# Order of the first attention job's start in a fused attention and expert kernel

## The chip, the cores and the metric

The kernel runs on one core of a Trainium2 chip. The metric is the device time of one execution in microseconds (us), as the median of several runs. The kernel before took 746.56 us (three runs, 745.12 to 747.57).

## What is computed

The reference is attention over 16 heads, followed by two feed-forward layers in float32. Cut to what matters:

```python
# q, k, v: (2, 8, 576, 64)
scores = scale * np.matmul(q, k.transpose(0, 1, 3, 2))
thresh = np.max(scores, axis=-1, keepdims=True) - tau
scores = np.where(scores >= thresh, scores, -1000000000.0)
scores = scores - np.max(scores, axis=-1, keepdims=True)
attn = np.exp(scores)
attn = attn / (np.sum(attn, axis=-1, keepdims=True) + 1e-09)
x = np.matmul(attn, v)                  # then as (1152, 512)
x = np.maximum(np.maximum(x @ w1, x @ w2), x @ w3) @ w_out
p = domain_probs / (domain_probs.sum(-1, keepdims=True) + 1e-09)
for e in range(4):
    out += p[:, e:e + 1] * (np.maximum(x @ m_w1[e], 0.0) @ m_w2[e])
```

The weights w1, w2, w3 and w_out come as 64-bit floats.

## The kernel before

Every float32 operand of a matmul is split in a high part (rounded by a copy on ScalarE) and the rest (a subtraction on VectorE or GpSimd), and products are summed over these parts. The program has three stretches. In the first (`attention_fast`) the eight heads of the first batch element are done as four jobs of two heads. In the second the other eight heads (`attention_slow`) are woven into the matmuls of the first three weight matrices. The rest is the expert layers, which are matmuls of one line, L832.

A job loads q, k and v of two heads (`load_job`, lines 129 and 130; the 64 rows over the 512 of a head are the tiles `qrem`, `krem`, `vrem`). `prep` transposes keys and queries on TensorE and splits them (K on ScalarE, L169, and VectorE, L171; QS on ScalarE, L178). The first job has its own forms: `load_first` (lines 140 to 142) and `prep_first`. There `head(h)` copies keys (L206), splits queries (L207, L208), transposes both (L214, L216) and splits the keys (L219, L221) and scales the queries (L220); between `head(0)` and `head(1)` the remaining 64 rows go through L226 to L237.

A job has nine steps (tiles of 128 query rows of a head, and one step for the remaining rows of both heads). A step's scores are four matmuls (`qk`, L301; eight for the step of the remaining rows). Then VectorE takes the negated row maximum (`peak`, L312) and a threshold (`limit`, L315), ScalarE the exponential (`power`, L319), VectorE the thresholding with the row sum (`weigh`, L324), GpSimd the division (`norm`, L332). TensorE transposes the result (`turn`, L342), it is split (`cut_hi` on ScalarE, L372, L375 and L379; `cut_lo`, L388 to L400) and multiplied by V (`gather`, L418). There are two PSUM buffers for scores, two of the kind T, and two of the kind U.

Beside this, `stream.flush(when)` writes out the preparation of weight blocks that is due at a count of matmul columns `when`. For 64-bit weights this is: load the words (L638, 512 KB each), exponent on ScalarE (L646), clamp on GpSimd (L656), and three integer operations on VectorE (L653, L659, L664). Then the block is stored for a second pass (L670) and split (L626, L630). Three such blocks are prepared during the first attention stretch with their own, early due times (`LAGS_FIRST`). `load_probs` loads the domain probabilities, which `norm_probs` uses long after.

In the first stretch the order of instructions on each engine is set by a scheduler of the language, which goes by priority and by its own idea of when something is ready. `tc.issue_after(x)` makes the instructions written inside it, on the engine of `x`, stand behind `x` in that engine's order. It adds no semaphore. Each engine executes its own list strictly in order. From the first L832 on, the order of the program text holds on TensorE, VectorE, ScalarE and GpSimd.

## Time and profile before

| what | before |
|---|---|
| median of three runs | 746.56 us |
| the profiled execution, its own time | 749.09 us |
| span of the profiled execution | 747.3 us |
| TensorE busy (share of the span) | 715.7 us (96%) |
| VectorE busy | 378.3 us (51%) |
| ScalarE busy | 339.0 us (45%) |
| GpSimd busy | 392.4 us (53%) |
| first L832 matmul | at 107.66 us |

The profile is one execution taken by the hardware profiler. Its views are the page (totals), a table of stretches (busy time of every engine between two times), the timeline (instructions in order of time), the waits and the chain of work that ended last. PE is TensorE, PEld its weight load, DVE is VectorE, ACT ScalarE, POOL GpSimd, SP the queue that issues most DMAs. A time in brackets with an arrow is how long the engine had been idle before an instruction, and what ended that.

### The profile page before, as it was taken

Reading aid. Unit: us, or ns where it says so; the run is one execution under the profiler, and the core shown is the slowest. Engines: PE = TensorE matmul, PEld = TensorE weight load, DVE = VectorE, ACT = ScalarE, POOL = GpSimd, SP = SyncE. Lnnn points to the kernel's source line nnn. Section 1 sums busy time; section 2 is a strip of 40 time slices with the busy share of each in tenths; the row PEclk is TensorE's granted clock in tenths of the full one; section 3 lists DMA queues with packets and bytes.
Section 4 is the critical chain, followed back from the end, with each engine's and each line's share of the span. In section 5 each row is a group of like instructions: output and inputs, shape, how many; then the busy total and the mean of one; then the engine's idle time right before and its main releaser. Section 6 shows DMA issues by size and latency. Waiting matters only on the chain.

```text
span 747.3 us, 11716 instructions
## 1 busy us (share of the span) xinstructions
PE 715.7 (96%) x4103; PEld 636.4 (85%) x4103; DVE 378.3 (51%) x900; ACT 339.0 (45%) x716; POOL 392.4 (53%) x435
## 2 busy tenths in 40 slices
PE   4798999999899999999999999999999999999997
PEld 3787889777688788888888899999998998998996
DVE  6798988775265765766766421112222222222222
ACT  5688984444544655465454412333321321321320
POOL 5789785777554555564564524544623522522520
PEclk9799999999999999999999999999999999999999
DMA  6702006876724124122322233223412313312303
GB/s 183 227 22 49 1 1 187 261 226 204 199 78 113 59 73 122 57 73 57 86 61 66 71 113 85 68 58 91 132 50 85 99 43 85 104 45 77 113 2 71
DMA packets 89369, 71.01 MB, mean 95 GB/s; under 512 B 24158, under 2 KB 75358, under 8 KB 89310
## 3 DMA queue, kind: packets, MB, share of 16 engines
q1 hardware_dynamic: 88860, 69.96, 32.7%
q8 instruction: 33, 0.54, 0.3%
q10 hardware_dynamic: 418, 0.30, 0.2%
q14 instruction: 26, 0.21, 0.1%
q0 software_dynamic: 32, 0.00, 0.0%
HBM read 61.59 MB, written 8.65 MB: 94 GB/s over the span
## 4 chain that ended last, share of the span: by engine, by line
PE 77%; DVE 5%; ACT 5%; POOL 5%; issue 3%; DMA 3%; SPq 1%; POOLq 0%; ACTq 0%; DVEq 0%
PE ps L832 63%; PE u L418 5%; PE s L301 4%; PE t L342 3%; POOL a L630 2%; DVE st_negm L312 1%; DMA vrem<-in_v_dram 1%; ACT em L319 1%; DMA words<-in_moe_w_dram 1%; POOL b L656 1%; PE u L175 1%; DMA krem<-in_k_dram 1%; DVE raw L664 1%; ACT a L626 1%; PE t L388 1%
## 5 line engine op out<-in xcount | busy, mean ns | idle before, releaser
L630 POOL TENSOR_TENSOR a<-raw,a 128x512 fp32r<-128x512 f32 (+1 forms) x116 | 145.1, 1256 | 163.6 <-ACT a L626 160.3
L832 PE MATMUL ps<-b,hh 128*128 128x512 f32 x576 | 184.3, 393 | 0.0
L832 PEld LDWEIGHTS ps<-b,hh 128*128 128x128 f32 x576 | 107.3, 188 | 20.4
L782 ACT ACTIVATE hh<-ps 128x320 fp32r<-128x320 f32 (+1 forms) x96 | 46.8, 488 | 152.3 <-PE ps L832 151.9
L832 PE MATMUL ps<-b,hl 128*128 128x512 f32 x288 | 113.1, 393 | 0.0
L832 PE MATMUL ps<-y1h,a 128*128 128x320 f32 x512 | 112.8, 309 | 0.0
L630 POOL TENSOR_TENSOR b<-raw,b 128x512 fp32r<-128x512 f32 x64 | 82.8, 1296 | 53.4 <-ACT b L626 53.4
L785 DVE SCALAR_TENSOR_TENSOR hl<-ps,hh 128x320 fp32r<-128x320 f32 (+1 forms) x96 | 53.4, 556 | 108.9 <-ACT hh L782 108.8
L626 ACT ACTIVATE a<-raw 128x512 fp32r<-128x512 f32 (+1 forms) x116 | 69.4, 612 | 58.8 <-PE ps L832 19.1
L801 DVE SCALAR_TENSOR_TENSOR acc<-ps,pr,acc 128x512 f32<-128x512 f32 x63 | 47.2, 749 | 80.4 <-PE ps L832 80.3
L832 PE MATMUL ps<-y0h,a 128*128 128x512 f32 x256 | 85.1, 403 | 0.8 <-POOL a L630 0.8
L832 PEld LDWEIGHTS ps<-y1h,a 128*128 128x128 f32 x512 | 85.4, 188 | 0.3
L319 ACT ACTIVATE em<-s,st_negm 128x576 f32<-128x576 f32 x72 | 53.3, 744 | 70.9 <-DVE st_negm L312 70.7
L332 POOL TENSOR_SCALAR em<-em,st_r,even 128x576 f32<-128x576 f32 x70 | 57.5, 824 | 43.2 <-DVE st_r L331 41.6
L832 PE MATMUL ps<-y1l,a 128*128 128x320 f32 x256 | 79.1, 309 | 0.0
L312 DVE TENSOR_REDUCE st_negm<-s 128x1 f32<-128x576 f32 x72 | 54.1, 753 | 48.9 <-PE s L301 48.4
L301 PE MATMUL s<-K,QS 128*128 128x288 f32 x320 | 59.7, 315 | 6.4 <-DVE em L324 3.2
L832 PE MATMUL ps<-x1h,a 128*128 128x320 f32 x288 | 63.4, 309 | 0.0
L324 DVE SCALAR_TENSOR_TENSOR em<-s,st_thr,em 128x576 f32<-128x576 f32 x72 | 58.2, 812 | 9.9 <-ACT em L319 7.8
L832 PEld LDWEIGHTS ps<-b,hl 128*128 128x128 f32 x288 | 54.1, 188 | 10.0
L301 PEld LDWEIGHTS s<-K,QS 128*128 128x128 f32 x320 | 49.8, 197 | 11.3 <-issue 6.0
L832 PEld LDWEIGHTS ps<-y0h,a 128*128 128x128 f32 x256 | 47.8, 191 | 9.6 <-POOL a L630 1.2
(129 smaller groups left out, 1271.1 us busy)
## 6 DMA issues: line engine op xcount, KB each, us to landing
raw<-in_moe_w_dram SPq DMA_DIRECT2D x128, 256.0 KB
words<-in_moe_w_dram SPq DMA_DIRECT2D x18, 512.0 KB
kept_w<-raw SPq DMA_DIRECT2D x18, 256.0 KB
raw<-kept_w SPq DMA_DIRECT2D x18, 256.0 KB
kraw<-in_k_dram SPq DMA_DIRECT2D x30, 128.0 KB
words<-in_moe_w_out_dram SPq DMA_DIRECT2D x8, 384.0 KB
vraw<-in_v_dram SPq DMA_DIRECT2D x8, 256.0 KB
qraw<-in_q_dram SPq DMA_DIRECT2D x7, 256.0 KB
```

The costliest lines, as they stand in the source:

```text
L301: nc.tensor.matmul(st.s[:, kh, 0:HS], lhsT=l, rhs=r, start=i == 0, stop=i == len(terms) - 1)
L312: nc.vector.tensor_reduce(out=st.stat["negm"], in_=views(st)[0], op=ALU.max, axis=AX.XY, negate=True)
L319: nc.scalar.activation(out=ev, in_=sv, func=AF.Exp, bias=st.stat["negm"])
L324: nc.vector.scalar_tensor_tensor(out=ev, in0=sv, scalar=st.stat["thr"], in1=ev, op0=ALU.is_ge, op1=ALU.mult, accum_out=st.stat["sum"])
L332: last = (nc.vector if swift else nc.gpsimd).tensor_scalar(out=em, in0=em, scalar1=re, scalar2=even, op0=ALU.mult, op1=ALU.add)
L418: at["valued"] = nc.tensor.matmul(pv, lhsT=l, rhs=r, start=i == 0, stop=i == len(terms) - 1)
L626: nc.scalar.activation(out=b["hi"], in_=b["raw"], func=AF.Copy)
L630: nc.gpsimd.tensor_tensor(out=b["lo"], in0=b["raw"], in1=f32(b["hi"]), op=ALU.subtract)
L782: nc.scalar.activation(out=hs[f][0][:, a:z], in_=ps, func=AF.Relu)
L785: nc.vector.scalar_tensor_tensor(out=hs[f][1][:, a:z], in0=ps, scalar=0.0, in1=f32(hs[f][0][:, a:z]), op0=ALU.max, op1=ALU.subtract)
L801: nc.vector.scalar_tensor_tensor(out=accs[t], in0=ps, scalar=pe, in1=accs[t], op0=ALU.mult, op1=ALU.add)
L832: nc.tensor.matmul(ps, lhsT=l, rhs=r, start=i == 0, stop=i == count - 1)
```

## The change

The remaining rows and the second head of the first job stand behind the first head's last scaling and last subtraction; the second head also stands behind the remaining rows' first instructions. The first step's `peak` and `power` are written right after `prep_first`. Everything that is written after that and before the end of the third pass of the loop (the second job's loads, the values, the weight preparation, later steps) stands, on its engine, behind these and behind each of the first steps' `power` and `weigh`. The due times of the early weight preparation are flushed in pieces (-53000, then -45900, -42500 and -READY after the first three steps' `weigh`) where it was all flushed before the first step. The values of the first job are queued one step later; the second job's `prep` starts one step later, and its loads are written before the loop. The domain probabilities' loads stand behind the last job's loads.

```diff
@@ load_job @@
-                nc.sync.dma_start(out=r[:, x, :], in_=src[b, 2 * p:2 * p + 2, MAIN:S, :])
+                last = nc.sync.dma_start(out=r[:, x, :], in_=src[b, 2 * p:2 * p + 2, MAIN:S, :])
             job.raw[nm] = (t, r)
+        at["loaded"] = last
+        return last
@@ prep_first @@
-            nc.scalar.activation(out=QS[:, qo:qo + MAIN], in_=tq, func=AF.Copy, scale=SCALE)
-            nc.vector.tensor_tensor(out=K2[:, ko:ko + MAIN], in0=tk, in1=f32(d1), op=ALU.subtract)
-
-        head(0)
+            sq = nc.scalar.activation(out=QS[:, qo:qo + MAIN], in_=tq, func=AF.Copy, scale=SCALE)
+            return sq, nc.vector.tensor_tensor(out=K2[:, ko:ko + MAIN], in0=tk, in1=f32(d1), op=ALU.subtract)
+
+        behind = ExitStack()
+        for x in head(0):
+            behind.enter_context(tc.issue_after(x.ins))
         split(QN[:, 2 * NC:], qr, kr[:, None])
...
-        nc.scalar.activation(out=k1r, in_=trk, func=AF.Copy)
-        nc.vector.tensor_tensor(out=k2r, in0=trk, in1=f32(k1r), op=ALU.subtract)
+        x1 = nc.scalar.activation(out=k1r, in_=trk, func=AF.Copy)
+        x2 = nc.vector.tensor_tensor(out=k2r, in0=trk, in1=f32(k1r), op=ALU.subtract)
         yield
-        head(1)
+        for x in (turned, x1, x2):
+            behind.enter_context(tc.issue_after(x.ins))
+        job.ready = head(1)
+        behind.close()
@@ attention_fast @@
         load_job(jobs[0], "v")
+        stream.flush(-53000)
         start = prep_first(jobs[0])
         next(start)
         qk(steps[0])
         for _ in start:
             pass
-        stream.flush(-READY)
-        back.add(values(jobs[0]))
+
+        begun = ExitStack()
+        for x in (peak(steps[0]), power(steps[0]), *jobs[0].ready):
+            begun.enter_context(tc.issue_after(x.ins))
+
+        begun.enter_context(tc.issue_after(load_job(jobs[1]).ins))
...
-                if st.r == LOAD_A:
+                if st.r == LOAD_A and i:
                     load_job(jobs[st.j + 1])
-                if st.r == PREP_A:
+                if st.r == PREP_A + (st.j == 0):
                     front.add(prep(jobs[st.j + 1]))
-            if st:
+            if i and st:
                 peak(st)
...
-            if nxt:
-                power(st)
+            if i and nxt:
+                raised = power(st)
+                if i <= 2:
+                    begun.enter_context(tc.issue_after(raised.ins))
+                if i == 1:
+                    back.add(values(jobs[0]))
...
-                weigh(st)
+                weighed = weigh(st)
+                if i <= 2:
+
+                    begun.enter_context(tc.issue_after(weighed.ins))
+                    stream.flush((-45900, -42500, -READY)[i])
...
+            if i == 2:
+                begun.close()
@@ at the end @@
-    plan.at(0, load_probs)
+    def load_probs_late():
+        with tc.issue_after(at["loaded"].ins):
+            load_probs()
+
+    plan.at(0, load_probs_late)
```

The names below are those of the program's tiles: kraw, krem, qraw, qrem, vraw and vrem are loaded rows, QN split queries, K and QS transposed keys and queries, s scores, st_negm, st_thr and st_sum a step's maximum, threshold and sum, em the exponentials, words, t, b and raw the weight preparation. The lines of the changed kernel are shifted by 2 to 26.

VectorE, from behind the scalar constant of tau at the very start, before:

```order
L206 COPY krem<-krem 128x64
L900 TENSOR_SCALAR even<-neg 128x1
L902 SCALAR_TENSOR_TENSOR ntau<-neg,tau_c 128x1
L208 TENSOR_TENSOR QN<-qraw,QN 128x4x64
L208 TENSOR_TENSOR QN<-qrem,QN 128x64
L206 COPY kraw<-kraw 128x4x64
L221 TENSOR_TENSOR K_135<-u,K_134 128x512
L208 TENSOR_TENSOR QN<-qraw,QN 128x4x64
L653 TENSOR_SCALAR t<-words 128x512
L232 TENSOR_TENSOR K_135<-t,K_134 128x2x64
L221 TENSOR_TENSOR K_135<-u,K_134 128x512
L653 TENSOR_SCALAR t<-words 128x512
```

and of the change, from the first head's query subtraction on:

```order
L210 TENSOR_TENSOR QN<-qraw,QN 128x4x64
L223 TENSOR_TENSOR K_137<-u,K_136 128x512
L208 COPY krem<-krem 128x64
L210 TENSOR_TENSOR QN<-qrem,QN 128x64
L236 TENSOR_TENSOR K_137<-t,K_136 128x2x64
L208 COPY kraw<-kraw 128x4x64
L210 TENSOR_TENSOR QN<-qraw,QN 128x4x64
L319 TENSOR_REDUCE st_negm<-s 128x1
L223 TENSOR_TENSOR K_137<-u,K_136 128x512
L322 TENSOR_SCALAR st_thr<-st_negm,ntau 128x1
L331 SCALAR_TENSOR_TENSOR em,st_sum<-s,st_thr,em 128x576
L675 TENSOR_SCALAR t<-words 128x512 x2
```

The copy of krem moved behind the first head's subtractions, the first maximum moved ahead of the second head's key subtraction, and both operations on words moved behind the first step's `weigh`; the second step's maximum comes next.

ScalarE, from the first query split on, before:

```order
L207 ACTIVATE QN<-qraw 128x4x64
L207 ACTIVATE QN<-qrem 128x64
L219 ACTIVATE K_134<-u 128x512
L207 ACTIVATE QN<-qraw 128x4x64
L220 ACTIVATE QS<-u 128x512
L231 ACTIVATE K_134<-t 128x2x64
L646 ACTIVATE b<-words 128x512
L219 ACTIVATE K_134<-u 128x512
L235 ACTIVATE QS<-t 128x2x64
L646 ACTIVATE b<-words 128x512
L220 ACTIVATE QS<-u 128x512
L246 ACTIVATE V<-vraw 128x8x64
```

and of the change:

```order
L209 ACTIVATE QN<-qraw 128x4x64
L221 ACTIVATE K_136<-u 128x512
L222 ACTIVATE QS<-u 128x512
L209 ACTIVATE QN<-qrem 128x64
L235 ACTIVATE K_136<-t 128x2x64
L209 ACTIVATE QN<-qraw 128x4x64
L242 ACTIVATE QS<-t 128x2x64
L326 ACTIVATE em<-s,st_negm 128x576
L221 ACTIVATE K_136<-u 128x512
L222 ACTIVATE QS<-u 128x512
L668 ACTIVATE b<-words 128x512 x2
L326 ACTIVATE em<-s,st_negm 128x576
```

The first exponential moved ahead of the second head's copies, of the exponents and of the values; before, it stood behind V and both VR.

SP, from the third load of words on, before:

```order
L638 DMA words<-in_moe_w_dram 128x4x256
L129 DMA qraw<-in_q_dram 128x2x256
L130 DMA qrem<-in_q_dram 128x1x64
L129 DMA kraw<-in_k_dram 128x4x64 x2
L130 DMA krem<-in_k_dram 128x1x64
L129 DMA kraw<-in_k_dram 128x4x64 x2
L130 DMA krem<-in_k_dram 128x1x64
L670 DMA kept_w_0_201<-raw 128x512
L638 DMA words<-in_moe_w_dram 128x4x256 x2
L129 DMA vraw<-in_v_dram 128x2x256
L130 DMA vrem<-in_v_dram 128x1x64
L847 DMA pr<-in_moe_domain_probs_dram 128x16
```

and of the change:

```order
L660 DMA words<-in_moe_w_dram 128x4x256
L130 DMA krem<-in_k_dram 128x1x64 x2
L130 DMA qrem<-in_q_dram 128x1x64
L660 DMA words<-in_moe_w_dram 128x4x256
L129 DMA qraw<-in_q_dram 128x2x256
L129 DMA kraw<-in_k_dram 128x4x64 x4
L660 DMA words<-in_moe_w_dram 128x4x256
L129 DMA vraw<-in_v_dram 128x2x256
L660 DMA words<-in_moe_w_dram 128x4x256
L130 DMA vrem<-in_v_dram 128x1x64
L692 DMA kept_w_0_251<-raw 128x512
```

The second job's small loads moved up, a load of words moved in between the second job's vraw and vrem, and the stores of prepared weights and the probabilities moved behind them.

## Rows read from the trace of the kernel before

**Rows 1.** Stretches: length, busy us (count) PE PEld DVE ACT POOL, clock, DMA, GB/s

```profile
20.00:30.00 10.00, 7.12 (x32) 6.25 (x32) 6.83 (x21) 5.71 (x11) 6.51 (x9) 0.54 0.82 257
30.00:40.00 10.00, 8.72 (x68) 7.86 (x67) 8.42 (x30) 9.48 (x23) 8.34 (x15) 1.00 0.59 154
40.00:50.00 10.00, 8.95 (x67) 8.29 (x68) 9.55 (x32) 8.37 (x19) 7.93 (x11) 1.00 0.07 23
...
140.00:150.00 10.00, 9.47 (x42) 7.52 (x41) 7.88 (x13) 5.06 (x10) 7.28 (x8) 1.00 0.85 265
```

**Rows 2.** Timeline to 12 us: start, us, engine, line, operation, [idle before <- releaser]

```profile
0.74 0.70 SPq L140 DMA_DIRECT2D kraw<-in_k_dram  x1
...
3.98 1.09 PE L214 MATMUL u<-ident,kraw 128*128 128x128 f32 x4 [3.98 <-DVE kraw L206]
...
5.11 0.15 DVE L898 TENSOR_SCALAR neg<-tau_c 128x1 f32<-128x1 f32 x1 [1.23 <-DMA tau_c<-in_tau_dram]
...
7.03 0.26 ACT L207 ACTIVATE QN<-qrem 128x64 fp32r<-128x64 f32 x1 [2.61 <-DMA qrem<-in_q_dram]
...
7.30 0.19 DVE L206 COPY krem<-krem 128x64 f32<-128x64 f32 x1 [2.04 <-DMA krem<-in_k_dram]
...
7.54 0.42 DVE L208 TENSOR_TENSOR QN<-qraw,QN 128x256 f32<-128x256 f32 x1
...
7.55 0.47 PE L226 MATMUL t<-ident,krem 128*128 128x128 f32 x1 [2.49 <-DVE krem L206]
...
9.17 0.60 ACT L220 ACTIVATE QS<-u 128x512 fp32r<-128x512 f32 x1 [1.09 <-PE u L216]
...
11.19 0.83 PE L301 MATMUL s<-K,QS 128*128 128x288 f32 x2
```

**Rows 3.** Timeline, 12 to 15 us: the first two steps' VectorE and ScalarE work

```profile
12.21 0.75 DVE L312 TENSOR_REDUCE st_negm<-s 128x1 f32<-128x576 f32 x1
...
12.88 0.69 DVE L659 SCALAR_TENSOR_TENSOR t<-b,t 128x512 uint32<-128x512 uint32 x1
...
13.50 0.74 ACT L319 ACTIVATE em<-s,st_negm 128x576 f32<-128x576 f32 x1
...
14.20 0.75 DVE L312 TENSOR_REDUCE st_negm<-s 128x1 f32<-128x576 f32 x1
...
14.87 0.81 DVE L324 SCALAR_TENSOR_TENSOR em<-s,st_thr,em 128x576 f32<-128x576 f32 x1
```

**Rows 4.** Timeline, 17 to 30 us: the second job's vrem and the fifth and sixth exponential

```profile
17.92 1.05 SPq L638 DMA_DIRECT2D words<-in_moe_w_dram  x2
...
19.60 0.56 SPq L130 DMA_DIRECT2D vrem<-in_v_dram  x1
...
24.98 0.76 DVE L312 TENSOR_REDUCE st_negm<-s 128x1 f32<-128x576 f32 x1
...
26.30 1.31 PE L301 MATMUL s<-K,QS 128*128 128x288 f32 x4
...
27.01 0.53 ACT L252 ACTIVATE VR<-vrem 64x64 fp32r<-64x64 f32 x2 [0.41 <-DMA vrem<-in_v_dram]
...
27.56 0.74 ACT L319 ACTIVATE em<-s,st_negm 128x576 f32<-128x576 f32 x1
...
28.34 0.82 DVE L324 SCALAR_TENSOR_TENSOR em<-s,st_thr,em 128x576 f32<-128x576 f32 x1 [2.35 <-ACT em L319]
...
28.68 0.28 ACT L379 ACTIVATE ar<-u 128x128 fp32r<-128x128 f32 x1
```

**Rows 5.** Timeline, 30 to 33 us: the sixth and seventh exponential, the eighth maximum

```profile
30.05 0.74 ACT L319 ACTIVATE em<-s,st_negm 128x576 f32<-128x576 f32 x1 [1.09 <-DVE st_negm L312]
...
32.12 0.30 ACT L189 ACTIVATE K<-u 128x128 fp32r<-128x128 f32 x1
...
32.91 0.79 ACT L319 ACTIVATE em<-s,st_negm 128x576 f32<-128x576 f32 x1
...
32.95 0.75 DVE L312 TENSOR_REDUCE st_negm<-s 128x1 f32<-128x576 f32 x1
```

More of the change, by code (lines that the diff above doesn't have):

```diff
@@ L219, in head @@
             nc.scalar.activation(out=d1, in_=tk, func=AF.Copy)
-            nc.scalar.activation(out=QS[:, qo:qo + MAIN], in_=tq, func=AF.Copy, scale=SCALE)
-            nc.vector.tensor_tensor(out=K2[:, ko:ko + MAIN], in0=tk, in1=f32(d1), op=ALU.subtract)
-        head(0)
+            sq = nc.scalar.activation(out=QS[:, qo:qo + MAIN], in_=tq, func=AF.Copy, scale=SCALE)
[3 more added lines that the diff above has]
+            behind.enter_context(tc.issue_after(x.ins))
         split(QN[:, 2 * NC:], qr, kr[:, None])
         tr = ptile_at("T", [P, 2, P])
-        nc.tensor.transpose(tr[:, 0, :], flat(kr), ident)
+        turned = nc.tensor.transpose(tr[:, 0, :], flat(kr), ident)
         nc.tensor.transpose(tr[:, 1, :], flat(QN[:, 2 * NC]), ident)
@@ L311, in peak @@
         st.stat = {x: atile([P, 1], F32, f"st_{x}") for x in ("negm", "thr", "sum", "r")}
-        nc.vector.tensor_reduce(out=st.stat["negm"], in_=views(st)[0], op=ALU.max, axis=AX.XY, negate=True)
+        return nc.vector.tensor_reduce(out=st.stat["negm"], in_=views(st)[0], op=ALU.max, axis=AX.XY, negate=True)
     def limit(st):
@@ L318, in power @@
         sv, _, ev = views(st)
-        nc.scalar.activation(out=ev, in_=sv, func=AF.Exp, bias=st.stat["negm"])
+        return nc.scalar.activation(out=ev, in_=sv, func=AF.Exp, bias=st.stat["negm"])
     def weigh(st):
         sv, _, ev = views(st)
-        nc.vector.scalar_tensor_tensor(
+        return nc.vector.scalar_tensor_tensor(
             out=ev, in0=sv, scalar=st.stat["thr"], in1=ev, op0=ALU.is_ge, op1=ALU.mult, accum_out=st.stat["sum"])
```

## Prediction

> **What bounds the kernel now.** I read three views. The table of stretches comes first [rows 1]. From 140 to 150 us TensorE is busy 9.47 of 10 us at the full clock of 2.4 GHz (granted share 1.00), and this is how the matmuls of L832 go on to the end. The first attention stretch is bound otherwise: ScalarE is the fullest engine from 30 to 40 us (9.48 of 10), VectorE from 40 to 50 us (9.55). Only the start has room. From 20 to 30 us VectorE has 6.83, ScalarE 5.71, and TensorE's clock is granted at 0.54, near 1.2 GHz. So the change can give or take only what the first 30 us leave idle. What it gives there reaches the end undiminished only if engines that are nine tenths full afterwards really are ahead in work, and not merely ahead in one chain.
>
> The timeline then shows where that idle time lies. VectorE reaches the copy of krem and sits 2.04 us until its load lands at 7.3; the query subtraction, whose operands came much sooner, stands behind it and starts at 7.54 [rows 2]. ScalarE waits 2.61 us for qrem in the same way, in front of the first head's key copy. The first maximum starts at 12.21, the first exponential at 13.50 and the first thresholding at 14.87 [rows 3]. Later ScalarE stands at VR for the second job's vrem, which was issued at 19.60 and lets ScalarE go on at 27.01. The fifth exponential is behind it, at 27.56, and VectorE idles 2.35 us for that one [rows 4].
>
> **The change, part by part.** *First step.* VectorE's query subtraction now needs only the three scalar operations on tau, from 5.11 on at some 0.15 each: 5.5 instead of 7.54. The four query transposes take about 1.1 as the key ones did [rows 2], 6.0 to 7.1; the scaling on ScalarE starts at 7.15 instead of 9.17. krem's landing at 7.3 is untouched: copy to 7.5, transpose (0.47) to 8.0, two score matmuls (0.83) to 8.9, the query remainder's transpose (0.4), two more (0.83), end at 10.1 instead of 12.02 [rows 2]. The first maximum starts at 10.1 and the first exponential at 10.9, 2.6 us sooner [rows 3]. The thresholding gains less, since VectorE has the second head's key subtraction in front of it, and ScalarE copies that head's keys only behind the exponential: 10.9 + 0.74 + 0.60, then 0.62 for the subtraction and 0.13 for the threshold, 13.0 instead of 14.87. VectorE stands idle from 10.85 to 12.25 meanwhile, which it did not before.
>
> *VectorE up to the fifth maximum.* From 13.0 its list holds four thresholdings (0.75 each from start to start), nine integer operations on weights (0.69 long; a maximum, 0.75 long, takes 0.67 from start to start [rows 3], so some 0.62), three maxima (0.67) and nine operations of about 0.1: 3.0 + 5.6 + 2.0 + 0.9 = 11.5, so the fifth maximum is at 24.5. Before it was at 24.98 [rows 4], with one more key subtraction (0.62) done by then. So the two words operations in front of the second maximum, and the idle 1.4 us, use up the head start: **VectorE is level there**, within 0.2.
>
> *ScalarE's wait for vrem.* By the same count the second block's last integer operation ends at 20.7; the words load that SP now issues ahead of vrem waits for it, so vrem is issued at about 21.5 instead of 19.60. How long it then takes is not shown. One bound is the 7.3 us that it took behind two words loads issued at 17.92 [rows 4], the other the 2.8 us of the very first load, issued at 0.74 and followed at 3.58 by the copy that frees the matmul at 3.98 [rows 2]. I take 4.0, a little under the middle: one words load instead of two directly ahead, and neither stores nor probabilities around it. It lands at 25.5. ScalarE should be there at 24.5. Behind the VR copies (0.53) come a weight copy, an exponent and a cut of about 0.6 each, and the fifth exponential is at 27.8, against 27.56. The sixth can follow at 28.5: its scores (1.31 at the low clock [rows 4]) run 26.2 to 27.5, the maximum to 28.2. Before, it was at 30.05, after 1.09 us idle [rows 5]. That is a lead of 1.55. Against it count one key copy (0.60) and a small cut (0.28 [rows 4]) not done yet, for one cut (0.6) done more: **ScalarE leads by 1.3** in work.
>
> For vrem, the Trainium skill, page "DMA: Bandwidth & Descriptors", section "Anatomy of one DMA — SWDGE (gpsimd) path", gives about 2.0 us fixed plus bytes at 436 GB/s, stated for GpSimd's path. As an estimate that is 2.1 us for these 32 KB, and the sum would gain 1.0 more, as ScalarE would not wait at all; the 7.3 us of the row disagree as soon as other loads stand in front.
>
> *What eats the lead.* In the new ScalarE list the second job's query scaling stands directly ahead of the seventh exponential. Its transposes stand in TensorE's list behind the eighth step's scores, which need the buffer that the sixth thresholding frees at 29.9. Scores and transposes then end between 31.3 and 32.3 (by clock), the scaling takes 0.6, and the seventh exponential is at 32.0 to 33.0, against 32.91 [rows 5]. Before, three more copies (32.12 to 32.91 [rows 5], 0.79) had been done by then, less one cut of 0.28. So on ScalarE the balance there is between a gain of 0.4 and a loss of 0.6; VectorE has its eighth maximum at about 32.0 instead of 32.95. Behind this all lists are reshuffled up to the stretch's end, with the same instructions.
>
> *The rest.* The probabilities' loads and the stores of prepared weights move back on SP; they are read only after the first stretch, so nothing waits, and if that were wrong SP and the DMA engines would still have time to spare behind 40 us, where the DMA share is 0.07 [rows 1]. No instruction is added or dropped on a computing engine.
>
> *Sum.* The lead in work is 1.3 at the sixth exponential and about 0 at the seventh on ScalarE, with VectorE some 0.9 ahead. I take the middle of 0 and 1.3: **0.6 us sooner** at the end of the stretch, and so at the end of the kernel. Against the profiled execution (749.09 us, span 747.3) that makes 748.5. That execution is 2.5 us above the median of the runs shown, 746.56, so the forecast for a median is 746.0. A difference under 0.3% (2.2 us) can't be told from none here.
>
> **The rivals.** *Faster.* The head start of the first exponential, 2.6 us, survives whole. For it: vrem may land after 2.8 us, 1.2 sooner than I take it, and the lead of 1.3 at the sixth exponential may stand, since the 2.35 us idle of VectorE and the 1.09 of ScalarE are just of this size. Together 2.5 to 2.6, time 744.0. Against it: VectorE's count up to the fifth maximum shows no lead, and the seventh exponential depends on TensorE. Chance 0.34.
>
> *Slower.* vrem takes 7.3 us again. Issued 1.9 us later it lands at 28.8, with the fifth exponential now behind VR and three more operations: 3.3 later than in the sum, so 2.7 slower than before, 749.3. It decides from a landing at 26.1 on (no gain left), and at 28.3 the loss passes 0.3%. For it: the DMA share from 20 to 30 us is 0.82 [rows 1], and a words load is put right before vrem. Against it: less is queued ahead. TensorE idle in that time would also get back its full clock later, as its clock is near 1.2 GHz in that stretch and at 2.4 GHz only with the dense work behind it [rows 1]; scores of a step at the low clock cost 0.5 more. Chance 0.21. The Trainium skill, "TensorE: Matmul & The Clock Gate", section "HAM oscillation — how this bites in real kernels", says that gaps filled by waits for DMA put the clock back. By that rule this case would lose somewhat more than 2.7.
>
> *The change doesn't do what it says.* The lists show that the first step is moved up, so this could only be in the rest of the stretch, where the scheduler's idea of readiness set an order that the chip doesn't meet. It gives a shift of the size of one stall, about 1 us either way, and lies within the forecast's own 0.45.
>
> **How the numbers follow.** Forecast (within 0.3%) 0.45 at 746.0, with a range of its own of 744.4 to 748.0; faster by over 0.3% 0.34 around 744.0; slower by over 0.3% 0.21 around 749.3. For 8 in 10 the range reaches 1.2 below the faster case, as the head start and a better later order can add, and up to 748.8, which leaves out about half of the slower case: 742.8 to 748.8.
>
> **What would show it.** Right: the query subtraction near 5.5, the first maximum near 10.1, the first exponential near 10.9, the fifth maximum within 0.5 of 24.5, the sixth exponential 1 to 2 us before 30.05, the first matmul of L832 about 0.6 sooner. Wrong: ScalarE idle over 2 us at VR on vrem (the slower rival), or the fifth maximum before 23 and the eighth before 31 (the faster one), or any shift that arises only behind 33 us.

## The result, and the profile after

The changed kernel takes 751.58 us (median; 750.63 to 752.62) where the kernel before, on the same chip, takes 746.70: a ratio of 1.0063, 95% interval 1.0045 to 1.0080. It is slower, by 3.4 to 6.0 us. The profiled execution of it took 750.8 us, with a span of 748.9; the engines are busy as long as before (TensorE 717.0 us for 715.7, ScalarE 338.2 for 339.0). The forecast was 746.0, with a range up to 748.8.

The start did what the lists promise. This is the timeline of the changed kernel from 4.5 to 15 us (columns as in [rows 2, 3]):

```profile
4.85 0.42 DVE L210 TENSOR_TENSOR QN<-qraw,QN 128x256 f32<-128x256 f32 x1
...
6.50 0.20 DVE L208 COPY krem<-krem 128x64 f32<-128x64 f32 x1 [0.16 <-DMA krem<-in_k_dram]
...
9.52 0.76 DVE L319 TENSOR_REDUCE st_negm<-s 128x1 f32<-128x576 f32 x1
...
10.31 0.74 ACT L326 ACTIVATE em<-s,st_negm 128x576 f32<-128x576 f32 x1 [1.18 <-DVE st_negm L319]
...
11.57 0.69 DVE L223 TENSOR_TENSOR K<-u,K 128x512 fp32r<-128x512 f32 x1 [1.30 <-ACT K L221]
...
12.42 0.82 DVE L331 SCALAR_TENSOR_TENSOR em<-s,st_thr,em 128x576 f32<-128x576 f32 x1
...
14.35 0.75 DVE L319 TENSOR_REDUCE st_negm<-s 128x1 f32<-128x576 f32 x1
```

The first maximum comes 2.7 us sooner than in [rows 3], the first exponential 3.2, the first thresholding 2.45. The second maximum is level already (14.35, 14.20 before). The next fence is the same timeline from 18 to 33 us, where [rows 4, 5] stood:

```profile
18.81 0.45 SPq L129 DMA_DIRECT2D vraw<-in_v_dram  x1
...
19.82 0.75 DVE L319 TENSOR_REDUCE st_negm<-s 128x1 f32<-128x576 f32 x1
...
20.39 0.56 SPq L130 DMA_DIRECT2D vrem<-in_v_dram  x1
...
23.65 0.63 ACT L253 ACTIVATE V<-vraw 128x512 fp32r<-128x512 f32 x1 [2.11 <-DMA vraw<-in_v_dram]
...
24.18 0.72 ACT L326 ACTIVATE em<-s,st_negm 128x576 f32<-128x576 f32 x1
...
24.94 0.82 DVE L331 SCALAR_TENSOR_TENSOR em<-s,st_thr,em 128x576 f32<-128x576 f32 x1 [1.68 <-ACT em L326]
...
25.76 0.74 DVE L319 TENSOR_REDUCE st_negm<-s 128x1 f32<-128x576 f32 x1
...
26.03 0.53 ACT L259 ACTIVATE VR<-vrem 64x64 fp32r<-64x64 f32 x2 [0.64 <-DMA vrem<-in_v_dram]
...
28.19 1.35 ACT L326 ACTIVATE em<-s,st_negm 128x576 f32<-128x576 f32 x2
...
32.22 0.60 ACT L180 ACTIVATE QS<-u 128x512 fp32r<-128x512 f32 x1 [1.53 <-PE u L177]
...
32.39 0.74 DVE L319 TENSOR_REDUCE st_negm<-s 128x1 f32<-128x576 f32 x1
...
32.71 0.74 ACT L326 ACTIVATE em<-s,st_negm 128x576 f32<-128x576 f32 x1
```

The fourth exponential, whose maximum ends at 20.57, stands behind V, which waits 2.11 us for vraw; VectorE waits 1.68 us for it. (The Trainium skill, "TensorE: Matmul & The Clock Gate", section "Architectural detail: the array is 16× 32×32, not 1× 128×128", says that ScalarE's queue is a strict FIFO. The trace agrees: 3.6 us from 20.57 to 24.18.) Still, at the seventh exponential the two kernels are level: 32.71, and 32.91 in [rows 5].

So the time is lost behind 33 us. The exponentials of the steps are good marks: the 17th, the 36th (the stretch's last), and then the first matmul of the expert layers. Timeline of the kernel before, then of the changed kernel:

```profile
60.05 0.75 ACT L319 ACTIVATE em<-s,st_negm 128x576 f32<-128x576 f32 x1
...
106.00 0.74 ACT L319 ACTIVATE em<-s,st_negm 128x576 f32<-128x576 f32 x1 [0.16 <-DVE st_negm L312]
...
107.66 0.39 PE L832 MATMUL ps<-x0l,a 128*128 128x256 f32 x1
```

```profile
61.87 0.75 ACT L326 ACTIVATE em<-s,st_negm 128x576 f32<-128x576 f32 x1
...
108.78 0.74 ACT L326 ACTIVATE em<-s,st_negm 128x576 f32<-128x576 f32 x1 [0.35 <-DVE st_negm L319]
...
110.67 0.39 PE L854 MATMUL ps<-x0l,a 128*128 128x256 f32 x1
```

From the seventh to the 17th exponential it was 60.05 - 32.91 = 27.14 us, and is 61.87 - 32.71 = 29.16: 2.0 lost. From the 17th to the first matmul it was 47.61 and is 48.80: 1.2 lost. Together with the 0.2 gained before, the matmuls begin 3.0 us later. (The 17th is a fair mark: around it ScalarE and VectorE run the same instructions in both kernels. The medians differ by 4.9 us, 3.4 to 6.0; these two executions don't show where the rest of that is lost.) The table of stretches shows idle time on ScalarE, which was full there [rows 1]:

```profile
20.00:30.00 10.00, 6.88 (x27) 5.73 (x28) 6.50 (x21) 7.21 (x15) 9.20 (x13) 1.00 0.97 314
30.00:40.00 10.00, 9.19 (x69) 8.15 (x69) 9.13 (x29) 6.93 (x17) 6.52 (x11) 1.00 0.24 56
40.00:50.00 10.00, 8.58 (x57) 6.86 (x58) 8.92 (x30) 8.73 (x22) 8.71 (x12) 1.00 0.17 44
...
140.00:150.00 10.00, 9.49 (x42) 7.54 (x41) 7.98 (x14) 4.74 (x9) 7.43 (x9) 1.00 0.77 252
```

ScalarE had 9.48 of 10 us from 30 to 40, and has 6.93; it had been 1.5 us ahead in busy time from 20 to 30. VectorE from 40 to 50 had 9.55, and has 8.92, but it has 0.7 more than before from 30 to 40, so for it this table alone shows no loss. From 140 us on nothing has changed. Where it happens can be seen on ScalarE between 34 and 42 us, in the changed kernel and then in the kernel before:

```profile
34.53 0.60 ACT L403 ACTIVATE am<-t 128x512 fp32r<-128x512 f32 x1 [0.26 <-PE t L402]
35.81 0.28 ACT L386 ACTIVATE ar<-u 128x128 fp32r<-128x128 f32 x1 [0.68 <-PE u L352]
35.98 1.37 ACT L326 ACTIVATE em<-s,st_negm 128x576 f32<-128x576 f32 x2
...
39.31 0.60 ACT L403 ACTIVATE am<-t 128x512 fp32r<-128x512 f32 x1 [0.57 <-PE t L402]
...
41.68 1.39 ACT L326 ACTIVATE em<-s,st_negm 128x576 f32<-128x576 f32 x2
```

```profile
35.27 0.74 ACT L319 ACTIVATE em<-s,st_negm 128x576 f32<-128x576 f32 x1
...
38.09 0.76 ACT L319 ACTIVATE em<-s,st_negm 128x576 f32<-128x576 f32 x1
...
39.94 0.75 ACT L319 ACTIVATE em<-s,st_negm 128x576 f32<-128x576 f32 x1
```

Before, exponentials come one at a time with cuts between them. Now the scheduler has put them in pairs (8 and 9, 10 and 11), behind cuts that wait for TensorE. At the tenth exponential 1.9 us are lost already (8.97 us from the seventh instead of 7.03; the eleventh, its pair, is level), and from the tenth to the 17th the two kernels take 20.19 and 20.11 us.

### The profile page after: what moved, and what is told of

Its sections match the earlier page's. It is cut to its first block, busy times and chain, and to the rows that moved or that the text cites. A ratio compares the mean times of both kernels' runs of the same rounds, so it can differ in the third digit from the quotient of the medians.

```text
span 748.9 us, 11729 instructions
## 1 busy us (share of the span) xinstructions
PE 717.0 (96%) x4103; PEld 635.6 (85%) x4103; DVE 378.9 (51%) x900; ACT 338.2 (45%) x716; POOL 392.7 (52%) x435
## 4 chain that ended last, share of the span: by engine, by line
PE 77%; ACT 6%; DVE 5%; POOL 5%; issue 3%; DMA 2%; SPq 0%; POOLq 0%; DVEq 0%; ACTq 0%
PE ps L854 64%; PE u L425 5%; PE s L308 4%; PE t L349 3%; POOL a L652 2%; ACT em L326 1%; DVE st_negm L319 1%; DVE em L331 1%; POOL em L339 1%; PE u L177 1%; POOL b L678 1%; ACT a L648 1%; DMA krem<-in_k_dram 1%; DMA vraw<-in_v_dram 1%; DVE raw L686 1%
## 5 line engine op out<-in xcount | busy, mean ns | idle before, releaser
L339 POOL TENSOR_SCALAR em<-em,st_r,even 128x576 f32<-128x576 f32 x70 | 57.8, 827 | 45.9 <-DVE st_r L338 43.7
```

The lines of the kernel that those rows point to most:

```text
L339: last = (nc.vector if swift else nc.gpsimd).tensor_scalar(out=em, in0=em, scalar1=re, scalar2=even, op0=ALU.mult, op1=ALU.add)
```

## Experiments

Four theories were tried. **A**: the changed order of the rest loses the time. **B**: the new start itself costs. **C**: the second job's loads, moved on SP's queue, cost. **D**: ScalarE's stand at V and VR sets the pace up to 30 us.

Most runs hold the lists: for each engine named, every instruction of the stretch is made to stand behind the one before it in a given list. Only the order is set; no wait is added or taken away, and every kernel computes the whole reference.

```diff
+    def in_order(orders):
...
+        for e, x in rank.items():
+            row = [named[e][y] for y in x if y in named[e]]
+            for u, v in zip(row, row[1:]):
+                tc.add_manual_dep(v, u.name, mybir.DependencyInfo(mybir.DependencyClass.NoSync, mybir.DependencyReason.DATA), reason="in_order")
+    in_order(ORDERS)
```

What differs between runs is the list in ORDERS, shown in short below. All results are in one table. Marks are from the profiled execution (us); the ratio is to the kernel before, timed on the same chip. The profiled execution of the kernel before (749.09 us) is 2.4 above its median, so marks and medians don't agree to better than some 2 us: the marks are read for the place of a loss, the ratios for whether there is one. A single mark also holds what an execution has won or lost by its first loads: changed_held has the changed kernel's lists, and it is 0.65 us later at the seventh exponential, much as it was at the first (10.99, 10.31), since krem had landed later. So times between two marks are compared where possible.

| kernel | 7th exp. | 7th to 17th | 17th to first matmul | first matmul | median | ratio, 95% interval |
|---|---|---|---|---|---|---|
| before | 32.91 | 27.14 | 47.61 | 107.66 | 746.70 | 1 |
| changed | 32.71 | 29.16 | 48.80 | 110.67 | 751.58 | 1.0063, 1.0045 to 1.0080 |
| changed_held | 33.36 | 29.17 | 48.82 | 111.35 | 750.95 | 1.0047, 1.0033 to 1.0062 |
| new_start_old_rest | 33.59 | 32.55 | 47.37 | 113.51 | 755.23 | 1.0104, 1.0087 to 1.0120 |
| old_start_new_rest | 32.33 | 30.94 | 48.79 | 112.06 | 752.99 | 1.0080, 1.0063 to 1.0097 |
| old_text_new_lists | 36.71 | 32.57 | 48.82 | 118.10 | 757.22 | 1.0130, 1.0115 to 1.0146 |
| prep_not_later | 33.73 | 29.63 | 47.65 | 111.01 | 752.27 | 1.0070, 1.0053 to 1.0088 |
| old_order_from_17 | 34.00 | 29.13 | 47.37 | 110.50 | 750.93 | 1.0053, 1.0031 to 1.0074 |
| start_alone | 35.45 | 27.07 | 47.37 | 109.89 | 748.71 | 1.0029, 1.0015 to 1.0043 |
| new_start_old_loads | 32.47 | 27.16 | 47.37 | 107.00 | 746.55 | 0.9995, 0.9984 to 1.0007 |
| old_start_new_loads | 33.85 | 27.12 | 47.65 | 108.62 | 750.02 | 1.0043, 1.0031 to 1.0056 |
| changed_old_loads | 32.96 | 29.14 | 48.76 | 110.86 | 752.11 | 1.0073, 1.0053 to 1.0092 |
| exp_ahead_before | 31.57 | 27.07 | 47.62 | 106.26 | 746.63 | 0.9985, 0.9973 to 0.9996 |
| exp_ahead_new_start | 31.40 | 27.08 | 47.37 | 105.85 | 746.91 | 0.9994, 0.9981 to 1.0007 |
| exp_ahead_changed | 31.32 | 29.14 | 48.80 | 109.26 | 751.55 | 1.0050, 1.0031 to 1.0070 |
| prep_not_later_free | 35.14 | 29.05 | 47.86 | 112.05 | 754.69 | 1.0086, 1.0068 to 1.0104 |
| two_exps_up | 35.59 | 31.97 | 48.79 | 116.35 | 755.27 | 1.0117, 1.0098 to 1.0135 |
| two_exps_up_held | 33.52 | 30.70 | 48.75 | 112.97 | 753.50 | 1.0081, 1.0067 to 1.0096 |
| two_exps_weigh_held | 32.44 | 33.90 | 48.77 | 115.11 | 756.49 | 1.0119, 1.0106 to 1.0133 |

**Start and rest crossed.** In the first two kernels the lists of VectorE, ScalarE and GpSimd up to 33 us are those of one kernel, and what is left stands in the order of the other; TensorE's and SP's lists are the scheduler's. In the third, the text of the kernel before gets these three lists from the changed kernel whole.

```diff
 ORDERS (changed kernel; VectorE, ScalarE, GpSimd)
   up to 8th maximum, 7th exponential: own list
-  rest: own list
+  rest: order of the kernel before
```

> The changed kernel, with the lists of VectorE, ScalarE and GpSimd held: as in the changed kernel up to 33 us (eighth maximum, seventh exponential), behind that what is left in the order that the kernel before has. TensorE's order is left to the scheduler, which follows. Theory A (the order of the rest costs the time): 744.5 to 747 us, first matmul of L854 between 105.5 and 108 us. Theory B (the new start leaves something behind that costs, such as late weights, a late second job or a low clock): 750 to 752 us as the changed kernel, first matmul near 110.7 us.

> The kernel before, with the lists of VectorE, ScalarE and GpSimd held: its own up to 33 us, behind that what is left in the order that the changed kernel has. Theory A: 749.5 to 752 us, first matmul of L832 between 109.5 and 111.5 us. Theory B: 746 to 747.5 us, first matmul near 107.7 us.

> The kernel before, with the whole lists of VectorE, ScalarE and GpSimd in the changed kernel's order, start and rest; the order in which tiles take buffers, and the loads, stay those of the kernel before. Theories A and B both: 750 to 752 us, as the changed kernel. If it comes near 746.7, neither holds, and the cost lies in TensorE's order, in the buffers or in the loads' queue.

The first came out at 755.23, far from either theory, the second at 752.99, on A's side and 1 us above its bounds, the third at 757.22, outside all of them. The times don't settle it. The likely reason is that a list that doesn't fit the text it stands in costs by itself: buffers are taken in the order of the text, and the old lists want the second job's keys a step sooner than the new text has them. The marks do settle one half. From the 17th exponential to the first matmul the old order takes 47.37 us in the new text, and the new one 48.79 and 48.82 in the old text.

**One part undone, and the old order late.** The next edit gives the first crossed kernel its buffers in the old order; the other takes the old order from the 17th exponential on.

```diff
-                if st.r == PREP_A + (st.j == 0):
+                if st.r == PREP_A:
```

> As the first experiment (the changed kernel's lists up to 33 us, the order of the kernel before behind that), and in the text the second job's preparation is not begun one step later, so that the buffers are taken in the order that the held lists want. If the 6 us that the first experiment lost between the seventh and the tenth exponential come from that step alone, they are gone: theory A 745 to 747.5 us, with the tenth exponential at 39 to 41 us. Theory B: 750 us or more.

> The changed kernel with its lists held up to the 17th exponential, at 62 us, and the order of the kernel before behind that on VectorE, ScalarE and GpSimd. From the 17th to the 36th exponential the three kernels with the new order took 46.9 us, the two with the old order 45.7 and 46.0. If the order alone makes this: 45.7 to 46.3 us from the 17th to the 36th exponential, and 750 to 751 us (0.7 to 1.2 under the changed kernel). If it depends on the state in which the stretch is reached: 46.9 us and 751 to 752 us.

The 32.55 us from the seventh to the 17th exponential become 29.63, so the later step made 3 us of that mismatch, but not all. The tenth exponential came at 42.31 and the time, 752.27, stands where B wants it. SP's list was free, and qraw went out at 15.13 us, later still than in the changed kernel (14.32); further down a late qraw is seen to cost by itself. The late order has a cost of its own: with the old one it is 47.37 us, 1.4 less than in the changed kernel. In the time (1.0053 against 1.0063) this can't be told from none.

**The new start alone.** The kernel before, with the lists of its four computing engines replaced up to the first thresholding; SP's is the scheduler's.

```diff
 ORDERS (kernel before; TensorE, VectorE, ScalarE, GpSimd)
-  up to first scores, exponential, thresholding: own list
+  up to first scores, exponential, thresholding: list of the changed kernel
   rest: own list
```

> The kernel before, with the lists of the four computing engines held: the changed kernel's order up to the first step's scores, first exponential, second head's copies and first thresholding; everything behind that in the order of the kernel before, on TensorE too. Theory A (the new start gains, the changed order of the rest loses): the head start of some 2 to 3 us at the first exponential shrinks on the way to a vrem that lands no sooner, and 0 to 2 us of it reach the end: 744.5 to 746.7 us. Theory B (the new start costs): over 748.5 us.

It is slower than the kernel before, which spoke for B. But the second exponential ran at 21.05, and the timeline shows why, with SP's rows for the same in the changed kernel behind it:

```profile
15.48 0.38 SPq L129 DMA_DIRECT2D qraw<-in_q_dram  x1
...
19.76 0.72 ACT L156 ACTIVATE QN<-qraw 128x256 fp32r<-128x256 f32 x2 [4.31 <-DMA qraw<-in_q_dram]
```

```profile
8.10 3.16 SPq L130 DMA_DIRECT2D krem<-in_k_dram  x2
...
11.35 1.94 SPq L130 DMA_DIRECT2D qrem<-in_q_dram  x1
...
14.32 0.45 SPq L129 DMA_DIRECT2D qraw<-in_q_dram  x1
...
19.00 0.72 ACT L158 ACTIVATE QN<-qraw 128x256 fp32r<-128x256 f32 x2 [1.62 <-DMA qraw<-in_q_dram]
```

In the kernel before, the same load goes out at 9.35 and the split runs at 15.17, after 0.17 us idle:

```profile
9.35 0.82 SPq L129 DMA_DIRECT2D qraw<-in_q_dram  x1
...
15.17 0.72 ACT L156 ACTIVATE QN<-qraw 128x256 fp32r<-128x256 f32 x2 [0.17 <-DMA qraw<-in_q_dram]
```

Once the first step stands ahead, the scheduler puts the second job's small loads and a load of words first, and qraw is issued 5 us later. (The length of an SP row is not the transfer's: 0.45 us, and ScalarE is released 4.2 us behind its end. The Trainium skill, "Perfetto Trace Analysis", section "DMA Instruction — HWDGE (DVE, Sync)", says that the recorded span ends when the sequencer is free again; the trace agrees.) That made theory C, and three runs with SP's list held as well:

```diff
 ORDERS, SP, behind the third load of words
-  qraw, qrem, kraw x2, krem, kraw x2, krem
+  krem x2, qrem, words (fourth), qraw, kraw x4
```

> The kernel before with all five lists held as they are, but for one piece of SP's: the second job's two krem loads, its qrem and the fourth load of words stand ahead of its qraw and kraw, as in the changed kernel. Theory C (the order of the loads costs: ScalarE's query split waits for a qraw that is issued some 5 us later): qraw issued near 14.5 us instead of 9.35, the second exponential, which stands behind its split, at 19 to 21 us instead of 16.46, and 748.5 to 751 us. Theory A (only the lists of the computing engines cost): 746 to 747.5 us.

> The kernel with the new start alone once more, with SP's list held as in the kernel before too (in the run before, the scheduler had put the second job's small loads, a load of words and two of the probabilities ahead of qraw, which came at 15.48 us and kept ScalarE waiting 4.31 us). Theory C: qraw issued near 9.5 us, no such wait, the second exponential before 16.5 us, 744.5 to 746.5 us, faster than the kernel before. Theory B (the new start itself costs): 748 to 749.5 us.

> The changed kernel with all five lists held as they are, but for SP's piece: the second job's qraw, qrem, kraw and krem in the order of the kernel before, ahead of the fourth load of words. Theory C: the query split at 15 to 16 us without the wait of 1.62 us, the third exponential 2 to 3 us before 20.30, and 747.5 to 750 us. If the lists of the computing engines hold the time whatever the loads do (theory A): 751 to 752 us.

C holds in the old lists. The loads' order alone costs the kernel before 0.94 us at every mark from the seventh on, and more if its sooner first exponential is counted (12.50 for 13.50); in time it costs 1.0043, which is 2.3 to 4.2 us. With it undone the new start is no longer slower, so B falls. Nor is it faster, as theory C wanted (0.9995, interval on both sides of 1): in the trace it leads by 0.4 us at the seventh exponential and by as much or more at every one behind it, which is less than the 0.65 between two executions of the same lists. C fails in the changed kernel: 752.11. There the third exponential came at 18.78 instead of 20.30, but V then waited 3.03 us for vraw instead of 2.11, and the fourth ran at 24.23 as before.

**ScalarE's stand at V and VR.** V and VR of the second job are first used behind that job's first exponential, the tenth, near 40 us; yet at 21 to 28 us exponentials that are ready stand behind them.

```diff
 ORDERS, ScalarE, kernel before (and new start)
-  V, VR x2, exponential 5
+  exponential 5, V, VR x2
 ORDERS, ScalarE, changed kernel
-  V, exponential 4, cut, VR x2, 3 more, exponential 5
+  exponential 4, V, cut, exponential 5, VR x2, 3 more
```

> The kernel before with all five lists held, but for one move on ScalarE: the fifth exponential, ready at 25.65 us, stands ahead of the second job's V and VR instead of behind them (27.56 us). If ScalarE's stand at vraw and vrem is what sets the pace up to 30 us (theory D): fifth exponential near 25.8 us, first matmul of L832 1 to 2 us before 107.66, 744.8 to 746 us, with the old start. If something else is late next (theory A, the whole order): 746.5 to 747.5 us.

> The new start with the old loads (746.55 us), and the fifth exponential ahead of V and VR as in the run beside it. VectorE has the fifth maximum 0.9 us later than the kernel before. Theory D: fifth exponential near 26.6 us, 745.7 to 746.5 us, thus no better than the old start with the same move. If the head start counts once the stand at vrem is gone: 744 to 745 us.

> The changed kernel with all five lists held, but for two moves on ScalarE: the fourth exponential ahead of V (it was ready at 20.5 us and ran at 24.18, behind a wait of 2.11 us for vraw), the fifth ahead of VR. Theory D: fourth exponential at 21.3 to 22 us, fifth at 24.5 to 26, first matmul of L854 at 108 to 109.5 us instead of 110.67, 749 to 750.3 us. Theory A (the order behind 30 us gives the time whatever comes before): 751 to 752 us.

The timelines of the first and of the third:

```profile
25.28 0.74 ACT L319 ACTIVATE em<-s,st_negm 128x576 f32<-128x576 f32 x1 [1.81 <-DVE st_negm L312]
...
31.57 0.74 ACT L319 ACTIVATE em<-s,st_negm 128x576 f32<-128x576 f32 x1
```

```profile
21.22 0.73 ACT L326 ACTIVATE em<-s,st_negm 128x576 f32<-128x576 f32 x1
...
24.69 0.74 ACT L326 ACTIVATE em<-s,st_negm 128x576 f32<-128x576 f32 x1 [0.45 <-DVE st_negm L319]
```

D holds for the traces in part: each kernel is 1.1 to 1.4 us ahead at the seventh exponential of the one it was made from, and keeps it to the first matmul (106.26, 105.85, 109.26). But not all of this comes from the move. At the last exponential in front of it (the fourth, the fourth and the third) they are already 0.49, 0.79 and 0.22 ahead, which leaves 0.9, 0.3 and 1.2 us for the move. All three times miss D's bounds (746.63, 746.91 and 751.55 for at most 746, 746.5 and 750.3), but the kernel before took 747.88 on that chip, so the ratios count. One move on one engine does for the kernel before what the whole change was to do: 0.9985 with an interval just below 1, the lowest here, 0.3 to 2 us under the kernel before. The new start adds nothing to it that the times show, and in the new start the move shows no gain in time (0.9994, and 0.9995 without it). The changed kernel stays at 751.55: it too gains at the start, and loses 2.0 and 1.2 us behind it all the same.

**The order the scheduler makes.** The changed kernel with the preparation where it was, and no list held.

> The changed kernel with the second job's preparation begun where the kernel before begins it, and nothing held: the scheduler makes a new order of the rest. If the later preparation is what costs: 746 to 748 us. If the order of the rest is a matter of luck: anything from 747 to 755 us, with another offset from exponential to exponential.

754.69, a ratio of 1.0086: taking this part back gains nothing, and may lose. The scheduler made a third order, with 29.05 and 47.86 us, behind a start that is 2.4 us later than the changed kernel's.

**What in the new order loses the 2.0 us.** The pairs of exponentials were the suspect.

```diff
 ORDERS, ScalarE, changed kernel
-  cut, cut, exponential 8, exponential 9 ... query split x3, exponential 10
+  exponential 8, cut, cut, exponential 9 ... exponential 10, query split x3
 ORDERS, VectorE (two_exps_up and two_exps_weigh_held alone)
-  maximum 9 ... thresholding 8; maximum 11 ... thresholding 10
+  thresholding 8, maximum 9 ...; thresholding 10, maximum 11 ...
```

> The changed kernel with its own lists held on VectorE, ScalarE and GpSimd but for two pairs of exponentials and thresholdings that are taken apart: the eighth exponential is moved ahead of two cuts and the tenth ahead of the third job's query split, each with its thresholding ahead of the next maximum. If the late eighth and tenth exponentials are what loses 2 us between 33 and 42 us: tenth exponential at 40 to 40.6 us instead of 41.68, first matmul of L854 0.5 to 2 us sooner than 110.67, 749.5 to 751 us. If another engine's wait is the cause: 751 to 752 us, as the changed kernel.

> The changed kernel with all five lists held, but on ScalarE the eighth exponential ahead of two cuts and the tenth ahead of the third job's query split; nothing else moved. If the late exponentials cost on their own: 1 to 2 us less from the seventh to the 17th exponential (29.16 us in the changed kernel, 27.14 in the kernel before), 749.5 to 751 us. If what waits for them stands in other lists as well: 28.5 to 29.5 us, 751 to 752 us.

> As the run beside it, and on VectorE the eighth thresholding ahead of the ninth maximum and the tenth ahead of the eleventh. If the pairs of exponentials and thresholdings are what costs: 27 to 28 us from the seventh to the 17th exponential, 749 to 750.5 us. If not: over 28.5 us.

> The changed kernel with its own five lists held, nothing moved. 750.5 to 752 us; first matmul of L854 between 110 and 112.5 us, with vrem landing 5 to 7.5 us behind its issue. A time outside 750 to 753 us would mean that holding lists has a price of its own.

The first told nothing, since TensorE's and SP's lists were free and vrem landed late; its rows are below. The held ones refute the suspicion: 30.70 and 33.90 us from the seventh to the 17th exponential instead of 27 to 28.2, and the first lies above the bounds of its other theory too. In the last, waits turn up all round, on ScalarE, TensorE and VectorE:

```profile
35.59 0.74 ACT L326 ACTIVATE em<-s,st_negm 128x576 f32<-128x576 f32 x1 [1.58 <-POOL em L339]
...
36.96 0.63 PE L349 MATMUL t<-ident,em 128*128 128x128 f32 x4 [1.02 <-ACT am L403]
...
42.61 0.60 ACT L403 ACTIVATE am<-t 128x512 fp32r<-128x512 f32 x1 [1.84 <-PE t L402]
```

```profile
45.25 0.29 DVE L407 TENSOR_TENSOR ar<-u,ar 128x128 fp32r<-128x128 f32 x1 [2.89 <-ACT ar L386]
```

Here the exponential that was moved up can't go ahead alone: it waits for a division on GpSimd (L339), and the cut (L403) that now stands behind it holds up TensorE. The changed kernel with its own lists held is at 750.95, within the interval of the kernel itself, so holding costs nothing.

What follows from the table as a whole: from the 17th exponential to the first matmul it is 47.37 to 47.65 us with the old order in nine kernels, 48.75 to 48.82 with the new one in nine. Start, loads and text make no difference to this, so these 1.2 us are shown to come from the order. From the seventh to the 17th it is 27.07 to 27.16 us in the six kernels that have the old order in the old text, and 29.13 to 29.17 in the five that have the new one unbroken in the new text (changed, changed_held, changed_old_loads, exp_ahead_changed, old_order_from_17). Start and loads make no difference to these 2.0 us either. But here order and text go together: the four kernels that cross them (the first three, and prep_not_later) are slower than both, at 29.63 to 32.57. So theory A is shown for the order together with the text it was made for, 2.0 + 1.2 = 3.2 us. That the order alone makes the 2.0, and which of its places does, stays open; taking the later preparation back doesn't undo the 2.0 (29.05, in the scheduler's third order). The times bear A out: changed_old_loads and new_start_old_loads have the new start and the old order of the early loads in common, and are at 1.0073 and 0.9995; with the exponentials moved ahead it is 1.0050 and 0.9994. Neither pair of intervals overlaps.

## Why the prediction was wrong

*First step*: right, and a little better than forecast (first maximum 9.52 for 10.1, exponential 10.31 for 10.9, thresholding 12.42 for 13.0), since tau's three operations and krem came 0.6 to 0.8 us sooner in this execution. VectorE's new idle time was there: 1.30 us.

*VectorE up to the fifth maximum*: 24.5 forecast, 25.76 measured. The count took VectorE as never waiting. It waited 1.68 us for the fourth exponential, behind V and vraw. The prediction had named only vrem.

*ScalarE's wait for vrem*: forecast to be issued at 21.5 and to land at 25.5; it was 20.39 and 26.03, so 5.6 us instead of 4.0, inside the bounds. (The estimate of 2.1 us from the Trainium skill, "DMA: Bandwidth & Descriptors", section "Anatomy of one DMA — SWDGE (gpsimd) path", disagrees with this too.) Fifth exponential 28.19 for 27.8, sixth 28.8 for 28.5 (it starts in the row x2 at 28.19).

*What eats the lead*: right. Seventh exponential 32.71 in 32.0 to 33.0, eighth maximum 32.39 for 32.0. Level, as said. It came out so although VectorE was 1.3 us late at the fifth maximum, which the prediction hadn't seen, so this is in part luck.

*The rest*: "nothing waits" was said of the probabilities and stores, and holds. But the second job's qraw, moved behind the small loads in the same queue, has no price anywhere in the sum. In the old lists it costs 0.9 us at every mark from the seventh exponential on, and 2.3 to 4.2 us in time; in the new ones it is hidden behind vraw.

*Sum*: 0.6 us sooner. The new start with loads and rest as before leads by 0.4 us in the trace, and by nothing that the times show (from 1.2 us faster to 0.5 slower). That is near the sum, but within what two executions differ by, and the loads aren't those that the sum counted with, so it doesn't confirm it. The step that failed is the sentence "Behind this all lists are reshuffled up to the stretch's end, with the same instructions", and the rival built on it, *The change doesn't do what it says*, which put "the size of one stall, about 1 us either way" on it and hid it in the forecast's own chance. Behind 33 us the traces lose 3.2 us, more than the whole difference of 3.0 at the first matmul, and the medians are 4.9 apart (3.4 to 6.0); the prediction had listed "any shift that arises only behind 33 us" as what would prove it wrong. The same instructions in another order, with the text that goes with it, took 78.0 us from the seventh exponential to the first matmul, where they had taken 74.8.

*The rivals*: the slower one had the sign, by another way. ScalarE's wait at VR on vrem was 0.64 us, not over 2, and no part of the loss against the kernel before comes from it, as the two are level at the seventh exponential. The faster one, a head start that survives whole, is refuted by new_start_old_loads.

## What to carry over

Where a scheduler sets the order, a fence at the start is an edit of every list behind it: compare those lists to the end of the stretch, and give a reshuffled order of full engines a range of several us, not a stall. Look for what a ready instruction stands behind on its in-order engine (here V, whose result isn't needed for some 15 us) before moving whole chains: one move was worth 0.3 to 1.2 us in the traces, the whole new start 0.4, which two executions of the same lists differ by as well. Marks along the stretch tell where time is lost, which end times don't. But a lead at one mark may be that of the execution: compare the time between two marks that both kernels reach with the same work done, and take an execution's offset from a mark that lies ahead of the edit.

## Not expected of the hardware

Three loads of 32 KB that follow each other at 8.1 us hold SP's queue for 1.6 to 1.9 us each (3.16 for two krem, 1.94 for qrem, above), where vrem, as large, takes 0.56 and qraw, of 256 KB, 0.45. Why is open. With them at the head, the DMA engines' share from 10 to 15 us is 0.27 instead of 0.70 (table of stretches of before, then of the changed kernel):

```profile
10.00:15.00 5.00, 2.81 (x13) 2.21 (x12) 4.47 (x10) 4.66 (x10) 3.58 (x7) 1.00 0.70 199
```

```profile
10.00:15.00 5.00, 3.80 (x14) 2.74 (x12) 3.67 (x8) 2.85 (x5) 1.19 (x2) 1.00 0.27 78
```

The landing of one and the same load differs by 1.8 us between kernels that issue the same loads in the same order on SP up to it: vrem took 5.6 us above, 5.5 in changed_held, and 7.4 in two_exps_up:

```profile
21.48 0.56 SPq L130 DMA_DIRECT2D vrem<-in_v_dram  x1
...
28.91 0.53 ACT L259 ACTIVATE VR<-vrem 64x64 fp32r<-64x64 f32 x2 [2.26 <-DMA vrem<-in_v_dram]
```

The granted clock of 1.00 in the changed kernel's stretch from 20 to 30 us can't be right: four score matmuls take 1.30 us there and 0.78 behind it, the two levels of 1.2 and 2.4 GHz, as in the kernel before (1.31 in [rows 4]).

```profile
22.03 1.30 PE L308 MATMUL s<-K,QS 128*128 128x288 f32 x4 [0.89 <-DVE em L331]
...
34.45 0.78 PE L308 MATMUL s<-K,QS 128*128 128x288 f32 x4
```
